# Attention and a two-layer feed-forward on one core: the weights' low bits on GpSimd, sums of |v| in six operations, a later output scale, and a new order of the first units

## The chip, the cores and the metric

The kernel runs on one core of a Trainium2 chip. The metric is the device time of one execution in microseconds (us). The kernel before took 600.85 us in the median of 3 runs (599.13 to 602.35). All data starts and ends in the device's HBM; the host only lays the arrays out.

The core has TensorE for matrix products (PE in the profile; PEld is the loading of its stationary operand), VectorE (DVE), ScalarE (ACT), GpSimd (POOL) and SyncE (SP), which issues the DMAs here. Each engine works through its own list of instructions in order; semaphores tie the lists together.

## The reference, cut to what matters

```python
scores = scale * q @ k.T                         # batch 4, heads 8, sequence 768, head size 64
keep = is_global | is_local                      # keys 0..7, and the last 96 positions
scores = where(keep, scores - slope[h] * dist, -1e9)
a = softmax(scores)
x = (a @ v) laid out as (4 * 768, 512)
h = x @ w_in                                     # 512 x 2048
g = maximum(h, 0) + alpha * minimum(h, 0)
out = g @ w_out                                  # 2048 x 512, float32
```

All inputs arrive as float32, but the two weight matrices are float64 in memory and the kernel makes its own operands of them. To keep float32's precision with 16-bit products, an operand is split into a high and a low float16 part, and a product is three matmuls: high by high, high by low, low by high.

## The kernel before, in words

**Units.** The 3072 tokens are 12 units of 256 tokens (u = 0 to 11, three for each batch entry b). A unit goes through attention for eight heads (`attend`), a transposition of its result x (`x_transpose`) and the feed-forward over 16 blocks f of 128 hidden columns: `ff_in` makes h and from it g in a high part gh and a low part gl, `ff_out` adds g's product to the output. Units 0 and 1 compute their attention in float32 (`score_pair`, and transposes on TensorE); later units split q, k, v and the probabilities and transpose through DMAs (`load_pair`, `split_pair`, `load_v`). Units 4 to 11 take the first product two blocks by two with seven products in place of eight (`seven`), out of sums of weight blocks that `sum_w` makes once.

**Weights.** `load_w` fetches the float64 words of a block f in two DMAs of 512 KB, and `split_w` turns each into a high and a low float16 part. The step touched by the change is in the middle of `split_w`. A float64 word has 64 bits; a float32 word is joined of its high half, shifted by three, and of the three bits below, which lie at the top of the low half. ScalarE makes two 16-bit halves of a tile `wb`: the upper from the word's high half (L576), the lower from bits of its low half (L578: a multiplication by 2 to the -13, with a constant tile `floor` as the bias so that the conversion to a whole number rounds down). VectorE joins them with the high half by a shift and an exclusive or (L583), into `wf` or, for the blocks that `sum_w` needs, into `words`. Then the float16 high part is rounded (L588 on VectorE, L587 on ScalarE, as the planner chooses), and the low part is what is left (L402). This happens 32 times, all in the first fifth of the kernel. Later every word is read again (`load_again`, `sizes`): a check that the weights lie in the range for which the splitting is made. It feeds `check` at the end, and if it fails, a general version runs.

**Scales.** For each batch entry `v_load`, `v_sums`, `v_most` and `v_range` bound the attention's result: a sum of |v| over the columns, the largest over the partitions (by a product on TensorE), and out of its exponent two powers of two: `vs`, by which x is scaled before it is split (L519 to L522), and `osc`, by which the output is scaled (L523 to L525). For b = 0 the sums are three reductions on VectorE of 1024 columns into two sums each (L486); for later b they are on ScalarE (L491).

**Order.** Nothing in the order is left to the run. Each operation has a key, its priority, in steps of one block f of a late unit (16 steps to a unit), and one or more ways: an engine, an estimated cost and the instructions. `Plan.order` simulates the five engines with these costs, picks on each free engine the ready operation with the lowest key, and lets an engine take an operation that is first another's when the queue there is longer than `FLEX` times its own cost. Buffers are given out in the order of keys. SP's operations are DMAs, with a cost of bytes / 330 per ns. The result is emitted as one fixed list for each engine. So a changed cost or key moves work all over the kernel. Keys that matter here: a unit's feed-forward block has `slot(u, f)`, its heads begin at `begin(u)` and follow each other by `step(u)`, the transposition comes `XAFTER` behind the last head, a weight's loads and splits lie `WL` and `WLEAD` before its first use, the second reading begins at `AGAIN`. `keep_busy` issues matmuls whose result nobody reads, at three places in the first units.

Of the kernel before, what the change touches and what calls it, by code (L numbers as in the profile page):

```python
# [146 lines left out]
class Plan:  # L147
# [37 lines left out]
    def order(self):  # L185
# [34 lines left out]
        while events:  # L220
# [11 lines left out]
            for e in engines:  # L232
# [28 lines left out]
                if isinstance(cost, Two) and free["POOL"] > now:  # L261
                    cost += SHARE * min(cost, free["POOL"] - now)
                if e == "SP":
                    dma = max(dma, now + 1125) + cost

                    busy, end = now + 525, dma
                    if self.way[i].__name__ == "transposes":
                        busy, end = now + 1245, dma + 500
                else:
                    end = busy = now + cost  # L270
# [25 lines left out]
def c_dve(n, fast=False, ptr=0):  # L296
    return (0.521 if fast else 1.042) * n + 68 + 57 * ptr
# [17 lines left out]
WIDE = 1  # L315
KP = 2
DP = 3.5
FLEX = {'ACT': 1, 'DVE': 1.5, 'POOL': 1}
GROUP = (2, 2, 2, 2)
# [6 lines left out]
WL = 3  # L326
WLEAD = 8
VS = 5
VL = 4
WARM = 9  # L330
FILL = 4
CHECK = 183
ENDING = 4
AGAIN = 60
LATE = 2000
# [7 lines left out]
SLOW, SLOWER = 1.06, 1.02  # L343
V1S, V1M, V1R = 5.5, 3, 1
STEP4 = 1.5
XAFTER = 3
# [9 lines left out]
def fast(tc, cn, a):  # L356
    nc = tc.nc
    ctx = ExitStack()
    with ctx:
# [101 lines left out]
        fin = fixed("fin", [P, 5])  # L461
        floor = fixed("floor", [P, 1])
        ends = fixed("ends", [P, 3, 512], F16)
        op("POOL", -100, 100, lambda: nc.gpsimd.memset(fin.t, 0.0), w=[fin])
        op("POOL", -100, 100, lambda: nc.gpsimd.memset(floor.t, 2.0**-14 - 0.5), w=[floor])
        op("POOL", -100, 1500, lambda: nc.gpsimd.memset(ends.t, 0.5), w=[ends])
# [12 lines left out]
        def v_sums(b, i, key):  # L479
# [4 lines left out]
            if not b:  # L484
                if i % 2 == 0:
                    op("DVE", key, c_dve(1024), lambda: v.tensor_reduce(  # L486
                        out=m.t[:, i : i + 2], in_=t.t, axis=AX.X, op=ALU.add, apply_absolute_value=True), r=[t], w=[(m, i)])
                return
# [18 lines left out]
        def v_range(b, key):  # L507
# [9 lines left out]
            def scale():  # L517
                big, x = e.t[:, 1:2].bitcast(I32), e.t[:, 2:3].bitcast(I32)
                v.tensor_scalar(out=x, in0=big, scalar1=23, scalar2=None, op0=ALU.logical_shift_right)  # L519
                v.tensor_scalar(out=x, in0=x, scalar1=-1, scalar2=266, op0=ALU.mult, op1=ALU.add)  # L520
                v.tensor_scalar(out=x, in0=x, scalar1=220, scalar2=None, op0=ALU.min)
                v.tensor_scalar(out=vs[b].t.bitcast(I32), in0=x, scalar1=23, scalar2=None, op0=ALU.logical_shift_left)  # L522
                v.tensor_scalar(out=x, in0=x, scalar1=-1, scalar2=254, op0=ALU.mult, op1=ALU.add)  # L523
                v.tensor_scalar(out=osc[b].t.bitcast(I32), in0=x, scalar1=23, scalar2=None, op0=ALU.logical_shift_left)
                v.tensor_scalar(out=osc[b].t, in0=osc[b].t, scalar1=1.0 / (WI * WO * KG), scalar2=None, op0=ALU.mult)  # L525

            op("DVE", key, 1150, scale, r=[e], w=[vs[b], osc[b]])

# [28 lines left out]
        def split_w(f, key):  # L557
# [3 lines left out]
            for part, raw in enumerate(raww[f]):  # L561
# [3 lines left out]
                else:  # L565
# [11 lines left out]
                    out=half(1), in_=hi_().bitcast(F32), mul=-(2.0**-60)), r=[raw], w=[(bits, 0)])  # L577
                op("ACT", k, c_act(n) + 209, lambda raw=raw, half=half: nc.scalar.activation(  # L578
                    out=half(0), in_=raw.t.bitcast(U16).rearrange("p (n t) -> p n t", t=4)[:, :, 1], func=AF.Identity,
                    bias=floor.t, scale=2.0**-13), r=[raw, floor], w=[(bits, 1)])  # L580
                wp = (w, f // 2 % 2) if kept else w
# [57 lines left out]

        def keep_busy(out):  # L640

            for n in range(FILL):
                nc.tensor.matmul(out[:, :P], lhsT=ident, rhs=ident, start=True, stop=True)
# [102 lines left out]
        def score_pair(u, h, key):  # L746
# [5 lines left out]
            def scores():  # L752
                if (u, h) == (1, 0):
                    keep_busy(sps[0].t)
                for qb, off, n, _, pc in windows(u):
# [4 lines left out]

            op("PE", key, 5 * 216 + 250 if u % 3 else 950, scores, r=[first[u, h][0]], w=sps)

        def attend(u, h, key):
# [50 lines left out]
            if plain:  # L814
# [13 lines left out]
                used = [pt, rv]  # L828
                cost = 207 * nb
            else:  # L830
# [84 lines left out]
        def x_transpose(u, qb, key):  # L915
# [28 lines left out]
            op("PE", key, 436, transposes, r=[xn[u]], w=[tp])  # L944
            if u == 0 and qb:
                x = buf("h", "busy", [P, UT])
                op("PE", key + 0.01, FILL * 214, lambda: keep_busy(x.t), r=[xn[u]], w=[x])
            mul(key, lambda: y.t[:, :NC, cols], tv, vs[0], [tp, vs[0]], [(y, qb)], "ACT", 512, True)
# [148 lines left out]
        def ff_out(u, f, key):  # L1097
# [6 lines left out]
            for t, half in ((0, None), (1, 0), (1, 1)) if u == NU - 1 else ((0, None), (1, None)):  # L1104
# [3 lines left out]
                def products(t=t, o=o, cols=cols):  # L1108
                    if u == f == t == 0:
                        keep_busy(o.t)  # L1110
                    tok = slice(128 * t, 128 * t + 128)
# [52 lines left out]
        for h in range(0, H, 2):  # L1164
            jobs.append((-90, load_first, (0, h)))
            jobs.append((-60 + h / 8, load_first, (1, h)))
        for u in range(NU):
# [17 lines left out]
        for f in range(NF):  # L1185
            jobs.append((2 * f - WL - WLEAD if f >= 8 else f - 61, load_w, (f,)))
            jobs.append((2 * f - WL, split_w, (f,)))
# [172 lines left out]
```

## Time and profile before

| | us |
|---|---|
| three runs, median (lowest to highest) | 600.85 (599.13 to 602.35) |
| the profiled execution, its own time | 601.47 |
| its span, first to last instruction | 599.7 |
| TensorE busy | 582.2 |
| VectorE busy | 500.6 |
| ScalarE busy | 421.3 |
| GpSimd busy | 82.3 |

The profile is of one execution. "Busy" is the time in which an engine has at least one instruction under way; matmuls are pipelined, and their ends are modelled, so a busy TensorE need not be at its peak. The granted clock is TensorE's, as a share of the full 2.4 GHz.

### The profile page before, as it was taken

What the parts mean: (1) busy time and instruction counts of PE and PEld (TensorE: products, weight loads), DVE (VectorE), ACT (ScalarE), POOL (GpSimd) and SP (SyncE); (2) the same over time, 40 slices, a digit from 0 to 9 for tenths busy, and PEclk for the clock granted to TensorE, in tenths of its full rate; (3) what the DMA queues carried; (4) which work ended last, traced back from release to release, by engine and by line L of the source; (5) the groups of instructions that cost most, each with busy time, mean ns of one, the idle gap of its engine ahead of it and who ended that gap; (6) DMA issues with size and microseconds to landing.
All of it is one profiled execution on the core that took longest, in us unless ns stands there. A gap on an engine that the chain in (4) does not pass through costs nothing.

```text
span 599.7 us, 16469 instructions
## 1 busy us (share of the span) xinstructions
PE 582.2 (97%) x6324; PEld 422.1 (70%) x6324; DVE 500.6 (83%) x1380; ACT 421.3 (70%) x1054; POOL 82.3 (14%) x161
## 2 busy tenths in 40 slices
PE   8899999999999999999999999999999999999995
PEld 6787666766766666677777777776677777777783
DVE  7899999997899698889879878889889878776442
ACT  6899999978788688767667667766667666641311
POOL 2001232433233332000000000000011000000000
PEclk9899999999999999999999999999999999999999
DMA  8988378257356569669977869588976947521001
GB/s 308 409 357 270 105 243 205 54 111 192 79 137 129 112 155 262 162 173 178 227 178 169 224 164 162 129 229 149 239 173 142 226 94 98 92 52 26 36 3 41
DMA packets 138919, 97.39 MB, mean 162 GB/s; under 512 B 115536, under 2 KB 115792, under 8 KB 138832
## 3 DMA queue, kind: packets, MB, share of 16 engines
q1 hardware_dynamic: 138832, 96.26, 65.0%
q8 instruction: 51, 0.84, 0.6%
q14 instruction: 36, 0.29, 0.2%
HBM read 58.22 MB, written 6.29 MB: 108 GB/s over the span
## 4 chain that ended last, share of the span: by engine, by line
PE 72%; DVE 16%; ACT 5%; DMA 3%; issue 3%; POOL 1%; SPq 0%; ACTq 0%; POOLq 0%; DVEq 0%
PE o L1113 32%; PE ha L1051 11%; PE hc L1051 8%; PE h L964 8%; PE av L863 5%; PE sp L741 3%; DVE pr L785 2%; ACT pr L795 2%; DMA xt<-xs 2%; DVE ps L402 1%; DVE ws L1008 1%; PE sp L758 1%; PE tp L820 1%; DVE g L977 1%; DMA raw<-in_qk_dram 1%
## 5 line engine op out<-in xcount | busy, mean ns | idle before, releaser
L1113 PE MATMUL o<-whl,gh 128*128 128x512 f16 (+1 forms) x800 | 230.2, 371 | 0.3 <-ACT os L1134 0.3
L1113 PE MATMUL o<-whl,gl 128*128 128x512 f16 (+1 forms) x400 | 148.2, 371 | 0.6 <-POOL gl L401 0.2
L1113 PEld LDWEIGHTS <-gh 128*128 128x128 f16 x800 | 71.5, 98 | 50.5 <-issue 3.3
L795 ACT ACTIVATE pr<-pr,sm 128x256 f32<-128x256 f32 (+1 forms) x176 | 85.5, 489 | 22.8 <-DVE sm L785 22.1
L1051 PEld LDWEIGHTS <-sw 128*128 128x128 f16 x1536 | 91.4, 98 | 12.0 <-issue 2.2
L964 PE MATMUL h<-xt,whl 128*128 128x256 f16 x768 | 92.8, 273 | 1.2 <-DVE g L977 0.7
L964 PEld LDWEIGHTS <-whl 128*128 128x128 f16 x768 | 74.4, 98 | 20.4 <-issue 3.2
L1051 PEld LDWEIGHTS <-whl 128*128 128x128 f16 x1152 | 70.9, 98 | 15.5 <-issue 1.9
L785 DVE CUSTOM_DVE_ANT_0 pr<-sp,D 128x256 f32<-128x256 f32 (+1 forms) x192 | 69.4, 393 | 6.2 <-PE sp L758 3.0
L1113 PEld LDWEIGHTS <-gl 128*128 128x128 f16 x400 | 39.1, 98 | 46.7 <-POOL gl L401 2.9
L401 POOL TENSOR_TENSOR gl<-g,gh 128x256 f16<-128x256 f32 x59 | 52.3, 886 | 110.7 <-ACT gh L979 103.2
L402 DVE SCALAR_TENSOR_TENSOR ps<-pr,ps 128x512 f16<-128x512 f32 (+1 forms) x80 | 56.4, 706 | 3.0 <-ACT ps L375 2.9
L1051 PE MATMUL ha<-xt,whl 128*128 128x128 f16 x768 | 53.2, 219 | 1.1 <-DVE gb L1062 0.8
L1051 PE MATMUL hc<-xt,sw 128*128 128x128 f16 x768 | 53.3, 219 | 0.5 <-DVE ga L1062 0.4
L1051 PE MATMUL ha<-xt,sw 128*128 128x128 f16 x768 | 53.4, 219 | 0.0
L803 POOL TENSOR_TENSOR fin<-fin,sm 128x4 f32<-128x4 f32 x40 | 11.9, 298 | 285.1 <-ACT pr L795 284.9
L375 ACT ACTIVATE ps<-pr 128x512 f16<-128x512 f32 (+1 forms) x77 | 44.8, 591 | 6.3 <-DMA pt<-ps 6.1
L375 ACT ACTIVATE gh<-ga 128x512 f16<-128x512 f32 x32 | 20.1, 628 | 39.8 <-DVE ga L1090 39.7
L863 PEld LDWEIGHTS <-pt 128*128 128x128 f16 x888 | 30.8, 98 | 5.4 <-issue 1.6
L375 ACT ACTIVATE x<-raw 128x672 f16<-128x672 f32 (+1 forms) x36 | 25.9, 726 | 11.6 <-PE sp L741 10.4
L795 ACT ACTIVATION_READ_ACCUMULATOR pr<-pr,sm 128x1 f32 x176 | 33.9, 192 | 0.0
L402 DVE SCALAR_TENSOR_TENSOR x<-raw,x 128x672 f16<-128x672 f32 (+1 forms) x40 | 33.3, 833 | 0.0
(150 smaller groups left out, 948.5 us busy)
## 6 DMA issues: line engine op xcount, KB each, us to landing
w<-in_w_dram SPq DMA_DIRECT2D x32, 512.0 KB, 8.9
again<-in_w_dram SPq DMA_DIRECT2D x32, 512.0 KB, 5.4
raw<-in_qk_dram SPq DMA_DIRECT2D x28, 336.0 KB, 3.6
out_dram<-os SPq DMA_DIRECT2D x23, 256.0 KB, 2.7
rawv<-in_v_dram SPq DMA_DIRECT2D x9, 512.0 KB, 5.4
raw<-in_qk_dram SPq DMA_DIRECT2D x12, 272.0 KB, 4.0
gp<-v SPq DMA_DIRECT2D x15, 192.0 KB, 3.1
first<-in_first_dram SPq DMA_DIRECT2D x4, 467.0 KB, 5.0
```

Of the source, the lines that this page charges most:

```text
L375: lambda: nc.scalar.mul(out=out(), in_=src(), mul=by.t if tile_ else by)),
L401: return e.tensor_tensor(out=out(), in0=src(), in1=hi(), op=ALU.subtract)
L402: return e.scalar_tensor_tensor(out=out(), in0=src(), scalar=val(), in1=hi(), op0=ALU.mult, op1=ALU.subtract)
L741: nc.tensor.matmul(sps[2 * n + i].t[:, pc : pc + m], lhsT=x.t[rows, qi, 128 * qb : 128 * qb + 128], rhs=x.t[rows, ki, 256 + off : 256 + of ...
L758: nc.tensor.matmul(sps[i].t[:, pc : pc + n], lhsT=qk_[:, 128 * qb : 128 * qb + 128], rhs=qk_[:, 256 + off : 256 + off + n], start=True, st ...
L785: op("DVE", key, c_dve(n) + 10, lambda qb=qb, n=n, dc=dc, pc=pc: v.tensor_tensor_reduce(out=pr.t[:, pc : pc + n], in0=sp.t[:, pc : pc + n] ...
L795: op("ACT", key + 1, c_act(n, ptr=1) + 93, lambda qb=qb, n=n, pc=pc: nc.scalar.activation(out=pr.t[:, pc : pc + n], in_=pr.t[:, pc : pc + ...
L803: op("POOL", key + 3, c_pool(2 * G), lambda: nc.gpsimd.tensor_tensor(out=fin.t[:, : 2 * G], in0=fin.t[:, : 2 * G], in1=sm.t[:, 2 * G : 4 * ...
L863: nc.tensor.matmul(out, lhsT=p_[:, 128 * j : 128 * j + 128], rhs=v_(j), start=m == 0, stop=m == len(ps) - 1)
L964: nc.tensor.matmul(hp.t, lhsT=w.t[:, wi, wc], rhs=x.t[:, NC * xi + c, :], start=n == 0, stop=n == 3 * NC - 1)
L1051: nc.tensor.matmul(out, lhsT=weight(name, f, wi, c), rhs=x.t[:, 8 * piece + m * xi + 2 * j + c, :], start=start and p == n == 0, stop=n == ...
L1113: nc.tensor.matmul(o.t[:, cols], lhsT=g_()[:, tok], rhs=w.t[:, wi, 512 + cols.start : 512 + cols.stop], start=f == 0 and n == 0, stop=f == ...
```

## The change

The lower halves of the 32 word tiles are made by GpSimd's `tensor_scalar` (a multiplication and a minimum) and no more by ScalarE's activation; the constant tile `floor` goes. The sums of |v| for b = 0 are six reductions of 512 columns into one sum each and no more three of 1024. The three operations that make the output scale become an operation of their own, six steps later in priority. In the planner a DMA ahead of step 20 counts 0.8 of its cost (its transposes excepted), and the costs of the first two units' scores and of their products with v are new. Constants of the order change: the distance of later weights' loads, the second reading of the weights 20 steps later, the spacing of heads from unit 4 on, the lead of the pairs' splitting, the sums of |v| for b = 1, the limit at which VectorE takes over work of ScalarE. `keep_busy` takes its number as an argument, four at each place as before, and the keys of the first loads are written with names of the same values.

```diff
...
                 if e == "SP":
+                    if ops[i][0] < FIRST and self.way[i].__name__ != "transposes":
+                        cost *= FIRST_RATE
                     dma = max(dma, now + 1125) + cost
...
-KP = 2
+KP = 1.5
...
-FLEX = {'ACT': 1, 'DVE': 1.5, 'POOL': 1}
+FLEX = {'ACT': 1, 'DVE': 2, 'POOL': 1}
...
-WLEAD = 8
-VS = 5
+WLEAD = 6
+VS = 6
...
-FILL = 4
+F1, F1S, W0, W0S = -60, 0.125, -61, 1
+CPOOL = 1000
+FILL_S, FILL_B, FILL_O = 4, 4, 4
+FIRST, FIRST_RATE = 20, 0.8
+UNSCALE = 6
...
-AGAIN = 60
+AGAIN = 80
...
-V1S, V1M, V1R = 5.5, 3, 1
-STEP4 = 1.5
+V1S, V1M, V1R = 6.5, 3, 1
+STEP4 = 1.7
...
-                if i % 2 == 0:
-                    op("DVE", key, c_dve(1024), lambda: v.tensor_reduce(
-                        out=m.t[:, i : i + 2], in_=t.t, axis=AX.X, op=ALU.add, apply_absolute_value=True), r=[t], w=[(m, i)])
+                op("DVE", key, c_dve(512), lambda: v.tensor_reduce(
+                    out=m.t[:, i : i + 1], in_=t.t[:, i % 2], axis=AX.X, op=ALU.add, apply_absolute_value=True),
+                   r=[(t, i % 2)], w=[(m, i)])
...
                 v.tensor_scalar(out=vs[b].t.bitcast(I32), in0=x, scalar1=23, scalar2=None, op0=ALU.logical_shift_left)
+
+            def unscale():
+                x = e.t[:, 2:3].bitcast(I32)
                 v.tensor_scalar(out=x, in0=x, scalar1=-1, scalar2=254, op0=ALU.mult, op1=ALU.add)
...
-            op("DVE", key, 1150, scale, r=[e], w=[vs[b], osc[b]])
+            op("DVE", key, 660, scale, r=[e], w=[vs[b], e])
+            op("DVE", key + UNSCALE, 490, unscale, r=[e], w=[osc[b]])
...
-                op("ACT", k, c_act(n) + 209, lambda raw=raw, half=half: nc.scalar.activation(
-                    out=half(0), in_=raw.t.bitcast(U16).rearrange("p (n t) -> p n t", t=4)[:, :, 1], func=AF.Identity,
-                    bias=floor.t, scale=2.0**-13), r=[raw, floor], w=[(bits, 1)])
+                low_ = lambda raw=raw: raw.t.bitcast(U16).rearrange("p (n t) -> p n t", t=4)[:, :, 1]
+                op("POOL", k, CPOOL, lambda low_=low_, half=half: nc.gpsimd.tensor_scalar(
+                    out=half(0), in0=low_(), scalar1=2.0**-13, scalar2=7.0, op0=ALU.mult, op1=ALU.min), r=[raw], w=[(bits, 1)])
...
-            op("PE", key, 5 * 216 + 250 if u % 3 else 950, scores, r=[first[u, h][0]], w=sps)
+            op("PE", key, 1100 + 214 * FILL_S * (u == 1 and h == 0) if u % 3 else 850, scores, r=[first[u, h][0]], w=sps)
...
-                cost = 207 * nb
+                cost = 112 * nb + 20
...
-            jobs.append((2 * f - WL - WLEAD if f >= 8 else f - 61, load_w, (f,)))
+            jobs.append((2 * f - WL - WLEAD if f >= 8 else W0 + W0S * f, load_w, (f,)))
```

## Rows read from the trace of the kernel before

**Rows 1.** Page, part 1, and part 4: the chain's shares by engine

```profile
PE 582.2 (97%) x6324; PEld 422.1 (70%) x6324; DVE 500.6 (83%) x1380; ACT 421.3 (70%) x1054; POOL 82.3 (14%) x161
...
PE 72%; DVE 16%; ACT 5%; DMA 3%; issue 3%; POOL 1%; SPq 0%; ACTq 0%; POOLq 0%; DVEq 0%
```

**Rows 2.** Busy time by stretch, all engines: stretch, length, busy (instructions), clock, DMA

```profile
10.00:30.00 20.00, 17.66 (x136) 15.46 (x136) 16.76 (x69) 17.61 (x41) 0.20 (x1) 0.91 1.03 408
...
50.00:70.00 20.00, 19.14 (x143) 13.02 (x141) 20.00 (x41) 18.89 (x39) 4.42 (x6) 1.00 0.74 240
...
70.00:125.00 55.00, 54.96 (x457) 37.40 (x455) 55.00 (x128) 52.88 (x122) 18.16 (x26) 1.00 0.57 147
...
220.00:250.00 30.00, 28.16 (x322) 20.12 (x321) 27.26 (x77) 26.99 (x77) 6.28 (x11) 1.00 0.97 244
...
590.00:599.70 9.70, 2.28 (x18) 1.57 (x16) 0.48 (x1) 1.13 (x2) 0.00 (x0) 0.87 0.19 63
```

**Rows 3.** Timeline, 26 to 28 us: start, us, engine, line, operation

```profile
26.32 0.15 DVE L523 TENSOR_SCALAR vmm<-vmm 128x1 int32<-128x1 int32 x1
...
26.59 1.13 PE L758 MATMUL sp<-first 64*128 64x256 f32 x8
...
27.16 0.42 DVE L879 TENSOR_TENSOR xn<-av,sm 128x256 f32<-128x256 f32 x1
```

**Rows 4.** Groups by shape, VectorE: count, busy us, mean ns, idle before

```profile
L486 DVE TENSOR_REDUCE vm<-vr 128x2 f32<-128x1024 f32 x3 | 3.6, 1212 | 0.0
```

**Rows 5.** Chain of waits, 11 to 17.3 us: start, us, what

```profile
12.00 0.83 issue
...
13.82 0.85 issue
...
16.24 0.67 ACT wb L576
```

**Rows 6.** Groups by shape, VectorE, 50 to 125 us

```profile
L583 DVE SCALAR_TENSOR_TENSOR wf<-w,wb 128x512 int32<-128x512 int32 x18 | 14.6, 810 | 0.0
...
L402 DVE SCALAR_TENSOR_TENSOR whl<-wf,whl 128x512 f16<-128x512 f32 x17 | 11.6, 687 | 0.0
...
L588 DVE TENSOR_SCALAR whl<-wf 128x512 f16<-128x512 f32 x9 | 4.5, 495 | 0.0
```

**Rows 7.** Busy time by stretch, line L578 alone

```profile
50.00:125.00 75.00, 19.00 (x23) 1.00 0.61 172
...
10.00:50.00 40.00, 8.55 (x10) 0.96 0.92 359
```

**Rows 8.** Line L401 on GpSimd: ns min/median/max, first and last start; who waited

```profile
L401 POOL TENSOR_TENSOR gl<-g,gh x59: 670/842/1327, 49.4 to 232.9; 128x256 f16<-128x256 f32 x59
...
  PEld L1113: 2.9, 6
```

**Rows 9.** Chain of waits, 49 to 67 us: shares by line

```profile
by line: DVE wf L583 28.6%; DVE whl L402 21.3%; issue 13.7%; DVE g L977 9.6%; DVE whl L588 8.3%; DVE words L583 6.7%; DVE xt L402 4.1%; PE h L964 3.3%; DVE gl L981 2.2%; PE av L863 0.7%; DVE sm L785 0.4%; DVE x L376 0.4%; DVE g L376 0.4%; D
```

**Rows 10.** Timeline, 58.5 to 59 us, VectorE and GpSimd

```profile
58.95 1.18 DVE L583 SCALAR_TENSOR_TENSOR wf<-w,wb 128x512 int32<-128x512 int32 x1
...
58.91 0.67 POOL L401 TENSOR_TENSOR gl<-g,gh 128x256 f16<-128x256 f32 x1 [2.30 <-ACT gh L979]
```

**Rows 11.** Line L583: duration in ns min/median/max

```profile
L583 DVE SCALAR_TENSOR_TENSOR wf<-w,wb x24: 654/684/1179, 18.0 to 122.8; 128x512 int32<-128x512 int32 x24
```

**Rows 12.** Tile xt's products on TensorE, and line L604

```profile
L1051 PE MATMUL ha<-xt,whl x768: 216/219/220, 231.5 to 585.5; 128*128 128x128 f16 x192
...
L604 ACT ACTIVATE size<-again x32: 661/675/691, 233.1 to 537.6; 128x512 f16<-128x512 f32 x32
```

**Rows 13.** Chain of waits, 212 to 246 us

```profile
233.11 0.66 ACT size L604
```

**Rows 14.** Chain of waits and timeline, 398 to 412 us

```profile
398.73 9.20 DMA xt<-xs
...
411.80 0.61 PE L1051 MATMUL ha<-xt,whl 128*128 128x128 f16 x8
```

More of the change, by code (lines that the diff above doesn't have):

```diff
@@ L461, in fast @@
         fin = fixed("fin", [P, 5])
-        floor = fixed("floor", [P, 1])
         ends = fixed("ends", [P, 3, 512], F16)
         op("POOL", -100, 100, lambda: nc.gpsimd.memset(fin.t, 0.0), w=[fin])
-        op("POOL", -100, 100, lambda: nc.gpsimd.memset(floor.t, 2.0**-14 - 0.5), w=[floor])
         op("POOL", -100, 1500, lambda: nc.gpsimd.memset(ends.t, 0.5), w=[ends])
@@ L638, in load_first, with keep_busy @@
                     firstv[u, h + i] = x, (lambda i=i: x.t[:, nk + 195 * i : nk + 195 * i + 195])
-        def keep_busy(out):
-            for n in range(FILL):
+        def keep_busy(out, fill):
+            for n in range(fill):
                 nc.tensor.matmul(out[:, :P], lhsT=ident, rhs=ident, start=True, stop=True)
@@ L753, in scores @@
                 if (u, h) == (1, 0):
-                    keep_busy(sps[0].t)
+                    keep_busy(sps[0].t, FILL_S)
                 for qb, off, n, _, pc in windows(u):
@@ L944, in x_transpose @@
             op("PE", key, 436, transposes, r=[xn[u]], w=[tp])
-            if u == 0 and qb:
+            if u == 0 and qb and FILL_B:
                 x = buf("h", "busy", [P, UT])
-                op("PE", key + 0.01, FILL * 214, lambda: keep_busy(x.t), r=[xn[u]], w=[x])
+                op("PE", key + 0.01, FILL_B * 214, lambda: keep_busy(x.t, FILL_B), r=[xn[u]], w=[x])
             mul(key, lambda: y.t[:, :NC, cols], tv, vs[0], [tp, vs[0]], [(y, qb)], "ACT", 512, True)
@@ L1109, in products @@
                     if u == f == t == 0:
-                        keep_busy(o.t)
+                        keep_busy(o.t, FILL_O)
                     tok = slice(128 * t, 128 * t + 128)
@@ L1165, in fast @@
             jobs.append((-90, load_first, (0, h)))
-            jobs.append((-60 + h / 8, load_first, (1, h)))
+            jobs.append((F1 + F1S * h, load_first, (1, h)))
         for u in range(NU):
```

## The prediction

> **What bounds the kernel now.** I read the page's busy shares first, then the busy time by stretch, then the chain of waits where TensorE is not full, and last the groups of the operations that the change touches. TensorE is busy 97% of the span, VectorE 83%, ScalarE 70%, GpSimd 14%, and the chain that ended last lies for 72% on TensorE [rows 1]. So time can be won only where TensorE waits or runs slowly, and the table by stretch shows where [rows 2]. From 10 to 30 us TensorE is idle 20 - 17.66 = 2.34 us, and its mean granted clock is 0.91: part of the stretch is at 1.2 and not 2.4 GHz, which costs about 0.09 x 20 = 1.8 us of full-speed work. From 50 to 70 it is idle 0.86 us, from 220 to 250 1.84, and 7.42 from 590 on, where the last outputs are evicted and written, which the change leaves alone. From 70 to 125 it is idle 0.04 us although VectorE is busy 55.00 of 55 and ScalarE 52.88: both vector engines are full there, yet TensorE always has something queued. This is the trap of the change: it unloads ScalarE mostly in a stretch where TensorE hardly waits.
>
> **The change part by part.** All sums are against the profiled execution's own 601.47 us (span 599.7 and 1.77 around it). It lies 0.62 above the median, 600.85; the same difference is taken off both.
>
> *The output scale later.* Three small operations (L523 to L525, 0.15 us each, from 26.32) stand on VectorE between the scale of v and what makes the first block ready for its transposes: 0.45 us leave that line [rows 3]. But the transposes wait for xn (27.16 + 0.42 = 27.58) and also for TensorE itself, which has the scores until 26.59 + 1.13 = 27.72 [rows 3]. The scores are the cover; worth 0 to 0.45, and I take 0.1, since xn ends only 0.14 before TensorE is free and 0.45 earlier would count only where the scores come earlier too.
>
> *Sums in six operations.* Three reductions of 1024 columns take 1212 ns each [rows 4]. In the chain two small operations sit behind such a reduction, for 0.83 and 0.85 us [rows 5]. Between halves a waiting operation can go in. No reduction of 512 columns is in the trace; half of 1212 is 606, and a two-input operation on 512 columns takes 684 in the median [rows 11], so six take 3.64 to 4.10 us against 3.64: up to 0.46 us more, in a stretch where VectorE is busy 16.76 of 20 us. If both waits shrink by half, 0.84 is gained; if both halves still run together, 0.46 is lost. I take 0.6 gained, near the rows of the chain, because each half is now a step of its own for the planner.
>
> *The low bits on GpSimd.* 32 operations leave ScalarE, 27.55 us in all: 8.55 (10 operations) from 10 to 50 and 19.00 (23, one cut by the edge) from 50 to 125 [rows 7]. GpSimd ran no such operation. Its subtraction with two inputs of 256 columns reads as many elements and takes 670 ns at least, 842 in the median [rows 8]; were an input of 512 columns as dear as two of them, 1684. So 0.67 to 1.68 us each; I take 1.0, near the median of the row, 32 us on an engine that is busy 82 of 600. The chain through a word gets no longer, for the operation now runs beside ScalarE's high half, which it followed before. Behind it on GpSimd queues the subtraction that makes gl, which TensorE reads 3.5 steps of the order later in the first units; all waits of TensorE's weight loads for gl are now 2.9 us [rows 8]. So I cost it at nothing; if those steps are not enough, each of some 25 subtractions in the stretch can be late by 1.0 us.
>
> Early, from 10 to 30, ScalarE is busy 17.61 of 20 us [rows 2], and TensorE loses 2.34 in idling and 1.8 in clock, 4.1 together. The low bits are part of what holds ScalarE up, but where the chain shows ScalarE's split, 0.67 us before the transposes of 17.28, it is the *high* half, L576 [rows 5], which stays. I give this part and the sums together half of the 4.1, 2.0 us: 0.6 above and 1.4 here. Bounds 0 and 3.5.
>
> From 50 to 70 the chain is on VectorE: joining the words (L583) is 28.6% of it and the rest of the split (L402) 21.3% [rows 9]. ScalarE's room helps there only where VectorE hands work over: nine roundings of the split (L588) of 4.5 us in all [rows 6] are free to go to ScalarE. Against this stands what GpSimd costs VectorE. The joining takes 684 ns in the median [rows 11] but 810 in the mean from 50 to 125 [rows 6], and the one that began at 58.95, just behind a subtraction of 0.67 us on GpSimd, took 1.18, 0.50 more [rows 10]. 18 x 0.126 = 2.3 us on 4.42 + 18.16 = 22.6 us of GpSimd [rows 2] is 0.10 us of VectorE for each us of GpSimd, the lower bound; 0.50 / 0.67 = 0.74 is the upper. 23 us more of GpSimd then cost VectorE 2.3 to 17 us; I take 0.25, or 5.8, nearer to the mean of many than to the single case. Hand-over and stretching nearly cancel on VectorE; what is left is ScalarE being earlier with its own. TensorE loses 0.9 us there, of which I take 0.6; bounds 0.9 gained and 6 lost.
>
> The Trainium skill, "GPSIMD Engine Reference", section "Specifications", says that GpSimd shares its SBUF interfaces with VectorE and contends with its instructions that have two SBUF inputs or run in a two-port mode: a rule against this change. The trace agrees for the joining (810 against 684 ns) and not for the rest of the split, which has two inputs as well and takes 687 in the mean [rows 6]. Section "Elementwise — side-by-side cycle accounting" of that page has 769 ns for 512 elements in the best case; by it GpSimd's part would be an estimated 25 us and not 32, and the stretching 4.4 and not 5.8.
>
> *The order.* The moved constants reach every unit. The second reading of the weights starts 20 steps later. A step is (585.5 - 231.5) / 127 = 2.79 us: from the first product of a seven-product unit to the last of the last one are seven units of 16 steps and 15 more [rows 12]. So 56 us later go 32 pairs of a 512 KB DMA on SP and an operation of 675 ns on ScalarE, with two on VectorE behind each. They start today at 233.1 [rows 12], just where the kernel goes over to seven products; the first of them is 0.66 us of the chain [rows 13], three of them fall in that stretch, 2.0 us of a ScalarE that is busy 26.99 of 30, with the DMA share at 0.97 [rows 2]. With them gone I take two thirds of TensorE's 1.84 us idle, 1.2; bounds 0 and 1.84. They come back at the end, when ScalarE is not needed much; a loss there would need the check of the weights to end after the last product. The heads of later units are spaced 1.7 instead of 1.5 steps, and their blocks are transposed 1.6 steps, 4.5 us, later. One such transfer now ends at 398.73 + 9.20 = 407.93, and its unit's products begin at 411.80 [rows 14]: 3.9 us of cover. 0.6 us a unit, 5 in eight, would show if no product of the unit before were left to fill in; I take 0, and 3 lost as the bound. The raw pairs are asked for half a step nearer to their use, and the loads of the later weights two steps; both pass the transposes in SP's queue at places that I can't see from here, so 0, with 1 us either way.
>
> The sum: 0.1 + 0.6 + 1.4 + 0.6 + 1.2 = 3.9 us; 601.47 - 3.9 = 597.6, and from the median 600.85 - 3.9 = 597.0.
>
> **The rivals.**
> *Nothing that can be measured.* (Within 0.5%, about 3 us, a measurement of this kernel can't be told from no change.) ScalarE's room falls where TensorE idles 0.04 us, later transposes take back the 1.2, and the first and second part alone are left, 0.7: 600.2. For it speaks the 97% on TensorE, against it the 4.1 us lost before 30.
> *A larger gain.* "Busy" may hide half-empty stretches. From 70 to 125 TensorE ran 457 matmuls, 8.3 per us; at that rate the 136 of 10 to 30 are 16.4 us and the 143 of 50 to 70 are 17.2 [rows 2]: 3.6 and 2.8 us lost, with the 1.84 at 220 together 8.2, though shapes differ. Three quarters of it are 6.2: 594.7.
> *Slower, by VectorE.* From 50 to 125 VectorE is full, 75.00 of 75 us [rows 2]. If GpSimd stretches it midway between the bounds, 0.42 for each us, its line ends 23 x 0.42 = 9.7 us later, and if the roundings stay on it, TensorE runs dry behind it by as much; the 3.3 us of the head and of 220 to 250 remain: 600.85 + 9.7 - 3.3 = 607.2. It decides from where the stretching less what is handed over exceeds 3.3 us. For it: the rows of the joining. Against it: the rest of the split shows no stretch [rows 6].
>
> **How the numbers follow.** Forecast 0.49, its own range 595.3 to 598.7; nothing 0.28; larger gain 0.12; slower 0.11. The range of 592.8 to 602.5 takes in the first three nearly whole and leaves out the slower case and a tail of the larger gain. Faster than 597.85 are the larger gain and 0.38 of the forecast's 0.49: 0.50. Slower than 603.85 is most of the slower case: 0.10. The rest is 0.40.
>
> **What would show it.** Right: ScalarE's total some 27 us lower and GpSimd's 32 higher [rows 1]; TensorE's idle time from 10 to 30 below 1.5 us with its clock above 0.91, and from 220 to 250 below 1 us; the mean of the joinings still above 800 ns, with fewer roundings on VectorE. Wrong: low bits above 1.4 us on GpSimd; TensorE idle by over 2 us between 50 and 125; the first product of a late unit waiting for a transposed block.

## The result: 0.8% slower, and the profile after

The changed kernel takes 605.37 us in the median of five runs (604.08 to 605.79), the kernel before 599.77 on the same chip; the ratio is 1.008, with an interval of 1.0055 to 1.0106. The forecast was 597.0 with a range to 602.5. It was wrong, on the side to which it gave 0.10. The profiled execution is one of 605.65 us, with a span of 603.9. Three single executions of the experiments below, of 670, 672 and 861 us at mean granted clocks of 0.85, 0.85 and 0.65, stand in no ratio.

First the page of the changed kernel, parts 1 and 4, to be laid beside [rows 1]:

```profile
PE 583.5 (97%) x6324; PEld 422.6 (70%) x6324; DVE 502.3 (83%) x1366; ACT 412.0 (68%) x1047; POOL 151.2 (25%) x184
...
PE 69%; DVE 14%; ACT 4%; issue 3%; POOL 1%; DMA 1%; DVEq 0%; ACTq 0%; POOLq 0%
```

GpSimd has gained 68.9 us, and not 32. ScalarE has lost 9.3, although 27.5 were taken from it; it has 1047 instructions for 1054, with 32 moved away, so the planner gave it 25 others. The moved operation itself, by its line (ns min/median/max, first and last start; below it who waited, us and times):

```profile
L587 POOL TENSOR_SCALAR wb<-w x32: 2095/2225/2621, 14.6 to 121.2; 128x512 uint16<-128x512 uint16 x32
...
  DVE wf L591: 3.8, 3
```

On ScalarE it took 861 ns (27.55 us for 32). The busy time by stretch (stretch, length, busy and count on PE, PEld, DVE, ACT, POOL, then clock, DMA share and GB/s), beside [rows 2]:

```profile
10.00:30.00 20.00, 18.52 (x144) 15.68 (x141) 17.63 (x75) 17.02 (x43) 9.58 (x6) 0.91 1.03 408
50.00:70.00 20.00, 16.50 (x101) 10.78 (x99) 15.42 (x26) 14.26 (x30) 18.41 (x10) 0.83 0.39 132
70.00:125.00 55.00, 51.84 (x435) 34.47 (x434) 54.13 (x116) 48.21 (x120) 50.80 (x35) 1.00 0.58 161
220.00:250.00 30.00, 29.19 (x316) 20.71 (x315) 27.31 (x74) 26.70 (x72) 9.57 (x14) 1.00 0.66 169
```

From 50 to 125 GpSimd is now the full engine: 69.21 of 75 us, 92%. VectorE, full before, is idle for 5.45 us. TensorE is idle for 3.50 + 3.16 = 6.66 us where it was idle for 0.90. At 10 to 30 it gained 0.86 us of idling and at 220 to 250 it gained 1.03. How far the work has come is read from the first product of unit 4 (beside [rows 12]; the second line is the second reading of the weights):

```profile
L1059 PE MATMUL ha<-xt,whl x768: 216/219/230, 239.1 to 591.0; 128*128 128x128 f16 x192
...
L612 ACT ACTIVATE size<-again x32: 655/676/688, 295.8 to 584.6; 128x512 f16<-128x512 f32 x32
```

Unit 4 begins at 239.1 instead of 231.5, 7.6 us late; from there to the end of the span it is 603.9 - 239.1 = 364.8 us instead of 599.7 - 231.5 = 368.2, 3.4 less. So the change loses early what it only half regains later.

Where the early loss arises is seen in the chain of waits of the changed kernel, here from 48 to 61 us and, below the second gap, from 88 to 94 (start, us, what; "issue" is time in which the engine waited for nothing that the profile shows):

```profile
48.43 2.29 POOL wb L587
50.72 0.35 issue
51.07 0.70 POOL wb L587
51.77 1.99 issue
53.76 1.01 POOL gl L407
...
54.82 1.89 PE o L1121 x4
56.71 4.71 PE h L972 x24
...
87.94 2.12 POOL wb L587
90.08 0.69 DVE wf L591
...
93.58 0.34 DVE g L985
```

The subtraction that makes `gl` stands behind low bits on GpSimd's fixed list; its timeline has three of them in a row before it:

```profile
45.91 7.77 POOL L587 TENSOR_SCALAR wb<-w 128x512 uint16<-128x512 uint16 x3 [0.77 <-DMA w<-in_w_dram]
53.76 1.00 POOL L407 TENSOR_TENSOR gl<-g,gh 128x256 f16<-128x256 f32 x1
```

The `gh` that it needs is ready at 50.67 (ScalarE's conversion of 0.41 us from 50.26), so `gl` is 3.1 us late. TensorE's own list has nothing before that product, and the next view, TensorE's timeline, shows the wait of 3.50 us and what follows it:

```profile
54.82 0.61 PE L1121 MATMUL o<-whl,gl 128*128 128x512 f16 x1 [3.50 <-POOL gl L407]
...
56.50 4.91 PE L972 MATMUL h<-xt,whl 128*128 128x256 f16 x24
...
62.54 2.78 PE L972 MATMUL h<-xt,whl 128*128 128x256 f16 x24
```

The same 24 matmuls take 4.91 us behind the wait and 2.78 later: the clock was at 1.2 GHz there (granted clock from 55 to 60 us: 0.50), and the mean from 50 to 70 is 0.83.

There is a second path. VectorE, which has to join the words and has a fixed list as well, stood idle for 0.86 us before the joining at 90.08 until the low bits were there. What TensorE needs of VectorE comes later by that, too: at 93.97 it has waited 1.57 us for `g`. Over the whole kernel TensorE's matmuls waited for (us, times, longest):

```profile
PE o L1121 <- POOL gl L407: 4.5, 4, 3.5
...
PE h L972 <- DVE g L985: 1.9, 2, 1.6
```

Of the 6.66 us from 50 to 125, 3.7 are waits for `gl` and 2.9 waits for VectorE.

### The profile page after: what moved, and what is told of

It is laid out like the page before. It is cut to its first block, busy times and chain, and to the rows that moved or that the text cites. A ratio compares the mean times of both kernels' runs of the same rounds, so it can differ in the third digit from the quotient of the medians.

```text
span 603.9 us, 16515 instructions
## 1 busy us (share of the span) xinstructions
PE 583.5 (97%) x6324; PEld 422.6 (70%) x6324; DVE 502.3 (83%) x1366; ACT 412.0 (68%) x1047; POOL 151.2 (25%) x184
## 4 chain that ended last, share of the span: by engine, by line
PE 69%; DVE 14%; ACT 4%; issue 3%; POOL 1%; DMA 1%; DVEq 0%; ACTq 0%; POOLq 0%
PE o L1121 33%; PE ha L1059 13%; PE hc L1059 10%; PE h L972 6%; PE av L871 3%; PE sp L749 3%; DVE whl L408 2%; DVE ps L408 1%; DMA xt<-xs 1%; DVE wf L591 1%; DVE g L985 1%; ACT pr L803 1%; DVE x L408 1%; DVE pr L793 1%; DVE ws L1016 1%
## 5 line engine op out<-in xcount | busy, mean ns | idle before, releaser
L803 ACT ACTIVATE pr<-pr,sm 128x256 f32<-128x256 f32 (+1 forms) x176 | 85.8, 490 | 17.3 <-DVE sm L793 16.8
L972 PE MATMUL h<-xt,whl 128*128 128x256 f16 x768 | 94.3, 276 | 2.0 <-DVE g L985 1.9
L811 POOL TENSOR_TENSOR fin<-fin,sm 128x4 f32<-128x4 f32 x40 | 14.6, 366 | 284.4 <-ACT pr L803 284.4
L587 POOL TENSOR_SCALAR wb<-w 128x512 uint16<-128x512 uint16 x32 | 73.8, 2307 | 19.9 <-DMA w<-in_w_dram 7.8
L407 POOL TENSOR_TENSOR gl<-g,gh 128x256 f16<-128x256 f32 x51 | 45.4, 892 | 61.6 <-ACT gh L987 47.9
L408 DVE SCALAR_TENSOR_TENSOR ps<-pr,ps 128x512 f16<-128x512 f32 (+1 forms) x80 | 55.0, 689 | 2.0 <-ACT ps L381 1.8
L381 ACT ACTIVATE ps<-pr 128x512 f16<-128x512 f32 (+1 forms) x78 | 46.4, 597 | 3.9 <-DMA pt<-ps 3.6
L381 ACT ACTIVATE g<-h,ak 128x256 f32<-128x256 f32 x60 | 27.8, 465 | 12.5 <-PE h L972 12.3
L985 DVE SCALAR_TENSOR_TENSOR g<-h,g 128x256 f32<-128x256 f32 x64 | 26.4, 414 | 10.5 <-ACT g L381 10.5
```

Of the source, the lines that this page charges most:

```text
L381: lambda: nc.scalar.mul(out=out(), in_=src(), mul=by.t if tile_ else by)),
L407: return e.tensor_tensor(out=out(), in0=src(), in1=hi(), op=ALU.subtract)
L408: return e.scalar_tensor_tensor(out=out(), in0=src(), scalar=val(), in1=hi(), op0=ALU.mult, op1=ALU.subtract)
L587: op("POOL", k, CPOOL, lambda low_=low_, half=half: nc.gpsimd.tensor_scalar(out=half(0), in0=low_(), scalar1=2.0**-13, scalar2=7.0, op0=AL ...
L803: op("ACT", key + 1, c_act(n, ptr=1) + 93, lambda qb=qb, n=n, pc=pc: nc.scalar.activation(out=pr.t[:, pc : pc + n], in_=pr.t[:, pc : pc + ...
L972: nc.tensor.matmul(hp.t, lhsT=w.t[:, wi, wc], rhs=x.t[:, NC * xi + c, :], start=n == 0, stop=n == 3 * NC - 1)
```

## Experiments

Ratios are to the kernel before, run on the same chip; the interval is 95%. The kernel before had medians of 599.77 to 599.93.

**Low bits back on ScalarE (all else as changed).**

```diff
-                op("POOL", k, CPOOL, ... nc.gpsimd.tensor_scalar(
+                op("ACT", k, c_act(n) + 209, ... nc.scalar.activation(
```

> The changed kernel with the low bits back on ScalarE; the six sums, the later output scale and all constants of the order stay. Theory 1 (the price of the operation: GpSimd takes 2.3 us for what the planner counts as 1.0, and is the bound from 50 to 125 us): the 6.7 us of TensorE's idle time from 50 to 125 fall to about 1, and the time to 596 to 601. Theory 2 (the new order itself is worse): it stays at 603 to 606, TensorE idle at the same places or others.

599.24 us, 0.9994 (0.9978 to 1.0009). With the low bits back the whole loss, 6.1 us to this kernel, is gone. All the rest of the change together is worth nothing that can be measured. Its stretches 10 to 30, 50 to 70 and 70 to 125:

```profile
10.00:30.00 20.00, 17.62 (x145) 15.00 (x145) 16.90 (x77) 17.73 (x47) 0.19 (x1) 1.00 1.03 409
50.00:70.00 20.00, 18.06 (x134) 11.98 (x131) 20.00 (x42) 19.61 (x38) 5.90 (x5) 1.00 0.65 218
70.00:125.00 55.00, 53.20 (x445) 36.24 (x443) 53.98 (x126) 52.23 (x121) 16.39 (x26) 1.00 0.60 159
```

TensorE's idle time from 50 to 125 is 3.74 us and not the 1 expected, so 2.8 of the 5.8 that the changed kernel adds are here too, in the new order with the low bits on ScalarE. They cost little: unit 4 begins at 232.7, 1.2 us later than before.

**Low bits on GpSimd alone, in the kernel before.**

```diff
-                op("ACT", k, c_act(n) + 209, ... nc.scalar.activation(
+                op("POOL", k, CPOOL, ... nc.gpsimd.tensor_scalar(
```

> The kernel before with one thing of the change: the low bits on GpSimd, counted as 1.0 us. Theory 1: slower by 4 to 8 us, 604 to 608, with GpSimd busy over 90% somewhere between 50 and 125 us. Theory 2: 599 to 601, as before.

610.95 us, 1.0196 (1.0166 to 1.0227), above the 604 to 608 expected: with the old constants the move costs twice as much. The operation takes 2314 ns, and the two stretches are:

```profile
50.00:70.00 20.00, 15.39 (x114) 10.84 (x113) 17.42 (x27) 15.21 (x31) 19.27 (x10) 1.00 0.48 159
70.00:125.00 55.00, 50.20 (x424) 33.36 (x422) 52.08 (x112) 40.88 (x102) 48.22 (x34) 1.00 0.53 143
```

TensorE is idle for 9.41 us at a full clock, with GpSimd busy for 67.49 of 75 us and VectorE idle for 5.5. Over this kernel its matmuls wait 4.2 us for VectorE's `g` and 2.4 for `gl`.

**The planner told the measured price.**

```diff
-CPOOL = 1000
+CPOOL = 2300
```

> The changed kernel with one number changed: the planner counts 2300 and not 1000 for the operation on GpSimd. If the loss comes from the planner's wrong count (lists of the engines in an order that GpSimd can't keep), it shrinks by half or more: 599 to 602. If GpSimd simply has too much to do from 15 to 125 us (74 us of low bits and 25 us of gl in 110), it stays at 603 to 606. Theory 2: 603 to 606 as well.

604.69 us, 1.0062 (1.0028 to 1.0096), but this is no single value: four runs of 599.2 to 599.8 at a mean granted clock of 0.998, two between, and five of 605.7 to 607.7 at 0.985 to 0.988. The gap goes with the clock: (0.998 - 0.986) x 605 = 7.3 us of full-speed work. Which of the two brings the other is not shown; in the changed kernel 605.37 us goes with a clock of 0.995 and 605.79 with 0.988. In the execution profiled, 599.70 us:

```profile
50.00:70.00 20.00, 17.94 (x134) 12.10 (x132) 18.40 (x37) 18.64 (x42) 18.80 (x9) 1.00 0.80 268
70.00:125.00 55.00, 52.70 (x437) 35.26 (x435) 54.39 (x115) 43.43 (x108) 50.13 (x36) 1.00 0.56 161
```

GpSimd is as full as in the changed kernel, yet TensorE is idle for 4.36 us and not 6.66: its matmuls wait 2.4 us for `gl` in place of 4.5. So in its better runs this kernel is rid of the loss with as much work on GpSimd, in another list, and there the wrong price in the planner is a part of the loss. In the median that is not shown: 604.69 lies in the 603 to 606 of the second case, five runs are as slow as the changed kernel, and the interval overlaps with that of its 1.008.

> The third experiment's kernel once more, for a second profile: its runs fell apart into 599 and 606, and the profile was of 599.7. If GpSimd's load lets TensorE's clock fall in some runs and not in others: a run near 606 shows stretches at the lower clock of some 13 us more than the 4.1 us at the end of the first profile, or a run near 599 shows none again.

One more execution of the same kernel took 599.12 us at 0.997, again with no stretch at the lower clock before the last outputs. No run near 606 has a profile, so what lets the clock fall in some of them stays open.

**What makes the operation dear.** The kernel goes through six forms in turn: as it is; input adjacent; 32-bit output; one operation and not two; both of the first two; float32 to float16. Most forms make other numbers than the reference; the one execution took 610.60 us.

```diff
+                if kind == 1:
+                    low_ = lambda raw=raw: raw.t.bitcast(U16)[:, :n]
...
+                if kind == 3:
+                    extra = dict(scalar2=None)
```

> What makes the operation dear: the changed kernel with six forms of it in turn over the 32 places (weights come out wrong in five of them). Form 0 as it is; 1 reads adjacent 16-bit numbers and not every fourth; 2 writes adjacent 32-bit numbers and not every second 16-bit one; 3 has one operation, the multiplication, in place of two; 4 is 1 and 2 together; 5 is float32 in, every second, to float16, one operation. If the stride of 16-bit numbers costs it, forms 1, 2 or 4 take 1.0 us or less; if the second operation, form 3 does; if neither, all take over 1.8 us.

GpSimd's groups by shape (count, busy us, mean ns, idle before); the first holds as it is, adjacent and one operation, the second the two with 32-bit output, the third the float form:

```profile
L602 POOL TENSOR_SCALAR wb<-w 128x512 uint16<-128x512 uint16 x17 | 37.3, 2194 | 14.1 <-DMA w<-in_w_dram 8.3 <-DMA raw<-in_qk_dram 2.8 <-DVE sm L834 1.0
L602 POOL TENSOR_SCALAR wb<-w 128x512 int32<-128x512 uint16 x10 | 20.5, 2050 | 1.4 <-ACT wb L584 0.7
L602 POOL TENSOR_SCALAR wb<-w 128x512 f16<-128x512 f32 x5 | 9.3, 1861 | 1.4 <-issue 1.1
```

By the single instructions, five or six of a form, the medians are 2.43 us as it is, 2.48 with adjacent input, 1.75 with one operation, 2.01 and 1.92 with 32-bit output (the second with adjacent input too), and 1.72 in the float form, which has one operation. So the second operation is the largest part that can be taken off, 0.68 us; an output of adjacent 32-bit numbers takes off 0.4 to 0.5, and adjacent input at most 0.1. No form comes near 1.0. The planner's own formula for GpSimd, 340 + 3.0 x 512 = 1876 ns, was nearer than the 1000 written in.

**The length of the operation alone.** Two kernels with the same lists: GpSimd's operation follows ScalarE's, which writes the whole word instead of its upper half (so the weights are wrong throughout, in both); only the columns that GpSimd reads differ, 184 or 512.

```diff
-                    out=half(1), in_=hi_().bitcast(F32), mul=-(2.0**-60)), r=[raw], w=[(bits, 0)])
+                    out=bits.t.bitcast(F32), in_=hi_().bitcast(F32), mul=-(2.0**-60)), r=[raw], w=[(bits, 0)])
...
-                    out=half(0), in0=low_(), ..., r=[raw], w=[(bits, 1)])
+                    out=half(0)[:, :SHORT], in0=low_()[:, :SHORT], ..., r=[raw, (bits, 0)], w=[(bits, 1)])
```

> The changed kernel with the low bits made for 184 of 512 columns (the others keep bits of the high half's float32, so the weights come out slightly wrong), which should take about 1.0 us on GpSimd, what the planner counts. For this ScalarE writes whole 32-bit words and GpSimd works behind it, not beside it; all lists are those of the next kernel. If the length of the operation is the whole error: joinings done by 124 us and not 129, TensorE idle under 2 us from 50 to 125, and 595 to 599, as forecast (3.9 us below before). If the use of GpSimd itself (its hold on VectorE, waits between engines) is a part: 600 to 604.

> The same lists with all 512 columns, 2.3 us each, behind ScalarE. As the changed kernel or worse, since the two halves now follow each other: 605 to 610. If it is at 600 or below, the order of this pair differs from the changed kernel's and the pair says nothing on it.

The short one takes 598.62 us, 0.9985 (0.9969 to 1.0), the full one 620.62, 1.0349 (1.0324 to 1.0374), more than the 605 to 610 expected. In the short one the last joining starts at 119.5 us, as expected, but TensorE is idle for 3.74 us from 50 to 125, as long as in the first experiment's kernel, and not for under 2. The short kernel's operation and its products of unit 4:

```profile
L588 POOL TENSOR_SCALAR wb<-w 128x184 uint16<-128x184 uint16 x32 | 34.3, 1072 | 36.1 <-ACT wb L585 27.5 <-DVE sm L794 4.4 <-DVE ps L409 2.7
...
L1060 PE MATMUL ha<-xt,whl x768: 216/219/229, 231.8 to 583.4; 128*128 128x128 f16 x192
```

and the full one's, with the line of h's product on TensorE (idle time before it at the end) and the wait for low bits before VectorE's work on tile `wf` (us, times):

```profile
L588 POOL TENSOR_SCALAR wb<-w 128x512 uint16<-128x512 uint16 x32 | 76.7, 2397 | 23.4 <-ACT wb L585 21.1 <-DVE vmm L526 0.4
...
L1060 PE MATMUL ha<-xt,whl x768: 216/219/229, 253.6 to 605.1; 128*128 128x128 f16 x192
...
L973 PE MATMUL h<-xt,whl 128*128 128x256 f16 x768 | 94.4, 276 | 9.3 <-DVE g L986 8.7
...
  POOL wb L588: 17.5, 16
```

With nothing but 32 x (2397 - 1072) = 42.4 us more on GpSimd, unit 4 begins 21.8 us later and the time is 22.0 us longer. In this form the loss is larger than in the changed kernel, where the operation runs beside ScalarE's, and the second path is the longer one: VectorE waits 17.5 us for low bits and TensorE 8.7 for VectorE's `g`, but only 3.4 for `gl`. The pair also says what the change would have been at the price that I forecast, in this form: 0.9 us faster than before (0 to 1.9), not 3.9.

**Is it the clock? TensorE kept busy in the wait.** 60 matmuls with zeros, which leave the sums as they are, are put where TensorE waits for `gl` at 51 us.

```diff
+                        if (u, f, t) == (0, 2, 0) and n in (0, 2):
+                            nothing(0 if n == 0 else 60)
```

> The changed kernel with 60 matmuls of a tile of zeros (128 columns, added to the output's sum, so that nothing changes in it) on TensorE between the two halves of the product that waits 3.5 us for gl at 51 to 55 us. All other lists are the same. If the 6.8 us at the lower clock from 54.0 are a price of that wait, and cost as much as they look (6.8 us at half speed, 3.4 us of work): the clock stays up there and the time falls by about 3, to 602. If the lower clock is hidden by later waits for GpSimd: 604.5 to 605.5 as before, with the clock up.

```profile
50.00:70.00 20.00, 17.93 (x170) 13.10 (x169) 16.25 (x27) 14.85 (x31) 19.28 (x10) 1.00 0.41 140
70.00:125.00 55.00, 51.34 (x421) 33.97 (x421) 53.53 (x115) 47.99 (x120) 50.74 (x36) 1.00 0.59 161
```

The clock stays at 1.00 there, and in this execution from 10 to 30 us too. The kernel takes 606.0 us, 1.0111 (1.0093 to 1.0129), no less than without. So the lost clock of the changed kernel is no term of its loss: unit 4 begins at 239.3 with the full clock and at 239.1 without.

**Fewer low bits on GpSimd.** Half of them, and then all with a free choice (ScalarE first, GpSimd at 2300), of which the planner gave GpSimd 12; and the second with 42 zero matmuls.

```diff
+                if not part:
+                  op("POOL", k, CPOOL, ...
+                else:
+                  op("ACT", k, c_act(n) + 209, ...
```

```diff
+                plan.op(k, [raw, floor], [(bits, 1)],
+                        ("ACT", c_act(n) + 209, ...),
+                        ("POOL", CPOOL, ...))
```

> The third experiment's kernel (2300 counted) with half the low bits back on ScalarE: 16 operations, one of a block's two, stay on GpSimd. Theory 1 (GpSimd has too much to do): its busy share from 50 to 125 falls from 92% to about 60%, the runs no longer fall apart into 599 and 606, and the time is 596 to 600. If any use of GpSimd there costs, by holding VectorE or by making TensorE's clock fall: 601 to 605.

> The low bits first on ScalarE, and on GpSimd (counted 2300) where ScalarE's queue is longer than that; the planner gives 12 of 32 to GpSimd. All else as changed. Theory 1: the best of the kernels, 596 to 599, with ScalarE below 52 of 55 us from 70 to 125 and GpSimd below 70%. If ScalarE's room is worth nothing there, as the first experiment's equal time suggests: 598.5 to 600.5.

> The kernel of the seventh experiment (12 of the low bits on GpSimd, the planner's choice) with 14 and 28 such matmuls of zeros in the same product, where it waits 0.9 and 1.6 us. If its 3.4 us at the lower clock from 56.6 cost 1.7 us: 597.7 against its 599.3, and so faster than the kernel before. If not: 599 to 600.

599.76, 599.32 and 599.44 us: 0.9994 (0.998 to 1.0008), 0.9992 (0.9979 to 1.0004) and 0.9998 (0.9986 to 1.001). With 16 of them GpSimd is busy 46.91 of 75 us (63%), and the loss is gone; but there is no gain either. ScalarE's room is worth nothing that can be measured here, at either dose, and the filled waits give nothing back.

**Sums and output scale alone, in the kernel before.**

```diff
+                op("DVE", key, c_dve(512), lambda: v.tensor_reduce(
+                    out=m.t[:, i : i + 1], in_=t.t[:, i % 2], ...
...
+            op("DVE", key + UNSCALE, 490, unscale, r=[e], w=[osc[b]])
```

> The kernel before with two things of the change: the six sums and the later output scale (the planner orders anew with these alone). By the prediction's steps 0.7 us faster, 599.2 against 599.9, with the clock from 10 to 30 us at 0.91 or above. If the pieces matter only through a new order, anything within 1.5 us of before either way.

601.44 us, 1.0023 (1.0004 to 1.0041), not the gain of 0.7. In the execution profiled, of 602.54 us, the clock from 10 to 30 is 0.83, below the 0.91 of before, and TensorE is idle there for 1.77 us instead of 2.34. Its runs part by the granted clock too: three of 598.3 to 598.7 at 0.997, nine of 600.7 to 603.3 at 0.991 to 0.993. The six reductions take 680 ns each, 4.0 us together.

**The second reading of the weights.** Back to step 60 in the first of these experiments' kernels (low bits on ScalarE), and to step 80 in the kernel before.

```diff
-AGAIN = 80
+AGAIN = 60
```

```diff
-AGAIN = 60
+AGAIN = 80
```

> The first experiment's kernel (low bits on ScalarE) with the second reading of the weights at its old place, step 60 and not 80. By the prediction's step it loses 1.2 us against that kernel, 600.4 and not 599.2, with TensorE's idle time from 220 to 250 us back from 0.9 to about 1.8. If the later reading is worth nothing: 599.2, idle time there about 0.9.

> The kernel before with one constant of the change, the second reading of the weights at step 80. By the pair of the first and eighth experiments (601.7 at 60, 599.2 at 80) about 2 us faster: 597.5 to 598.5. If the later reading is only worth something together with the other constants: 599.3 to 600.5.

The first: 601.70 us, 1.0032 (1.0017 to 1.0046), 2.5 above the kernel with 80. The second: 598.01, 0.9975 (0.996 to 0.999), 1.5 us faster than before. From 220 to 250 us, the stretch named for it, the kernel before with 80 has TensorE idle for 0.23 us in place of 1.84:

```profile
220.00:250.00 30.00, 29.77 (x337) 21.49 (x335) 27.98 (x78) 27.09 (x80) 7.95 (x14) 1.00 0.74 170
```

In the other pair the gain lies elsewhere. The first experiment's kernel, with step 80, and the same with 60:

```profile
220.00:250.00 30.00, 29.10 (x329) 21.37 (x328) 26.74 (x78) 27.76 (x81) 8.22 (x14) 1.00 0.62 137
250.00:590.00 340.00, 339.88 (x4209) 249.03 (x4206) 277.03 (x777) 207.19 (x534) 16.20 (x48) 1.00 0.66 148
...
220.00:250.00 30.00, 28.55 (x327) 20.94 (x325) 27.56 (x80) 27.08 (x78) 6.96 (x12) 1.00 0.83 197
250.00:590.00 340.00, 337.68 (x4190) 246.75 (x4188) 275.76 (x777) 205.69 (x534) 16.90 (x50) 1.00 0.66 141
```

TensorE is idle for 1.45 us and not 0.90 from 220 to 250, but for 2.32 and not 0.12 from 250 to 590.

**A version that beats both.** At step 80 with 3.5 steps between readings the last three of the 32 get keys behind the step that takes the maximum over all of them: in the changed kernel that maximum is taken at 564.9 us and the last comparison comes at 585.7. So the kernel's check of the weights' range leaves out the last three tiles, a fault of the change that its time does not show. The spacing is brought down so that all 32 lie before it.

```diff
-AGAIN = 60
+AGAIN = 80
...
-RATE = 3.5
+RATE = 3.15
```

> The kernel before with the second reading of the weights from step 80 on, each 3.15 and not 3.5 steps after the last, so that its last comparison lies at step 181.7, ahead of the check at 183. As the eleventh experiment, 597.5 to 598.5, and 1 to 2 us faster than before. If the closer spacing costs ScalarE or the DMAs something: 599 to 600.

596.61 us (594.65 to 597.15), 0.9938 (0.9913 to 0.9963), 3.3 us faster than before where 1 to 2 were expected. The last operation of its second reading on ScalarE starts at 555.0, and unit 4 to the end takes 595.4 - 232.5 = 362.9 us:

```profile
L1051 PE MATMUL ha<-xt,whl x768: 216/219/230, 232.5 to 582.5; 128*128 128x128 f16 x192
...
L604 ACT ACTIVATE size<-again x32: 652/672/684, 288.4 to 555.0; 128x512 f16<-128x512 f32 x32
```

## Why the prediction was wrong

*The step that failed* is the price of the low bits: "So 0.67 to 1.68 us each; I take 1.0". They took 2.31 in the mean, 2.10 at least, above the upper bound. Both bounds came from a subtraction with two inputs of 256 columns. The reading behind the lower one and behind the 1.0, that the cost goes by the elements read, was false: one input of 512 columns costs 2.1 to 2.6 us with two operations and about 1.75 with one (the six forms). The upper one, 842 x 2 = 1684, goes by the elements written; it is close for one operation, and the 0.68 us of the second was left out. The Trainium skill, "GPSIMD Engine Reference", section "Elementwise — side-by-side cycle accounting", has 769 ns for 512 elements in the best case; the trace has 2307, so that for this operation the measurement decides against it.

*"So I cost it at nothing"* fell with the price. 74 us of low bits must pass GpSimd between 14.6 and 124 us, with `gl` behind them in the same list. The cover of 3.5 steps was gone: TensorE's weight loads wait for `gl` for 7.1 us, where it was 2.9 [rows 8], and its matmuls for 4.5, where it was 0.2. The sentence itself had the mechanism ("each of some 25 subtractions in the stretch can be late by 1.0 us") and left it out of the sum and of the rivals. The second path, VectorE waiting in its own list for low bits (3.8 us here, 17.5 in the kernel with 512 columns behind ScalarE), is in no step of the prediction. That the length of the operation is enough for a loss is shown by the pair with 184 and 512 columns; that the planner's 1000 makes part of it, only by the better runs of the kernel with 2300, which are level with before. Both signs that I had named for this, low bits above 1.4 us and TensorE idle by over 2 us from 50 to 125, came.

*VectorE stretched by GpSimd*, the rival on the slower side, had the sign and not the mechanism. It wanted joinings slower and VectorE full. The groups on VectorE from 50 to 125 us, beside [rows 6]:

```profile
L591 DVE SCALAR_TENSOR_TENSOR wf<-w,wb 128x512 int32<-128x512 int32 x17 | 13.1, 774 | 4.1 <-POOL wb L587 3.8 <-ACT wb L584 0.3
L408 DVE SCALAR_TENSOR_TENSOR whl<-wf,whl 128x512 f16<-128x512 f32 x17 | 12.9, 768 | 0.1
...
L596 DVE TENSOR_SCALAR whl<-wf 128x512 f16<-128x512 f32 x4 | 2.4, 607 | 0.0
```

With three times the work on GpSimd (69.21 us, not 22.58) the joining takes 774 ns, less than the 810 of before; the rest of the split rises from 687 to 768 and the rounding from 495 to 607. So the means show no stretching of the joining and 17 x 0.081 = 1.4 us for the split, and VectorE now waits 3.8 us for the low bits. The test that I had written, joinings still above 800, came out against me; fewer roundings on VectorE, 4 for 9, came out right.

The single instructions of the two traces say what the means hide. Without an operation of GpSimd beside it, no joining into `wf` and no rest of its split took over 0.70 us in either kernel. Beside one, five of 10 joinings took 1.10 to 1.18 us before, and in the changed kernel three of 21 took over 1.0. The rest of the split ran beside GpSimd in 7 of 24 cases before, one of them of 0.83 us, and in 23 of 24 after, seven of them of 0.88 to 1.15. So the split had seemed unstretched in [rows 6] because it seldom met GpSimd, and my price for each us of GpSimd, 0.10 to 0.74, does not carry over from one of its operations to another.

*ScalarE's room, 1.4 + 0.6 us.* TensorE's idle time from 10 to 30 did fall below 1.5 (to 1.48), but the clock stayed at 0.91. With the low bits still on ScalarE the first experiment's kernel had a clock of 1.00 there, with 2.38 us idle, so the 1.8 us for the clock did not hang on the low bits. With 12, 16 or 32 cheaper low bits away from ScalarE no kernel shows a gain beyond 0.9 us. The opening remark, that the change unloads ScalarE where TensorE hardly waits, should have been given more weight than the busy shares of the head.

*The sums and the output scale, 0.7 us.* Not shown: alone they measure 1.4 slower, in runs that differ by the granted clock. Their size, up to 0.46 us more on VectorE, was right (4.0 us for 3.64). "No reduction of 512 columns is in the trace" was not: L539 of the kernel before is one, of float16, and took 675 ns, near the 680 measured.

*The later second reading, 1.2 us.* Right in sign and too small: TensorE's idle time at 220 to 250 fell to 0.81, and the step is worth 1.5 to 2.5. The place was right for the kernel before; in the new order most of the gain lies behind 250 us. *Later heads at nothing* held: with the reading back at 60 and all other constants moved, unit 4 to the end takes 600.2 - 232.2 = 368.0 us, and 368.2 before.

The sum as measured, in the two executions profiled: 7.6 us lost before unit 4 and 3.4 won behind it, 4.2 of span (the medians of the five runs are 5.6 apart).

## What to carry to other kernels

An operation that an engine has never run in the trace has no price from a row that resembles it in elements; where another operation stands behind it on a full path, the rival "this engine becomes the bound" is to be worked out above the upper price too (here 2.31 us for 1.68), with the operations on other engines that wait for its result. Before moving work off an engine ask whether the engine that everything waits for is idle in that very stretch: here it was for 0.9 us of 75, and no more could be won there at any price. A wrong price in a planner can cost twice, in the engine's time and in a list that puts the urgent operation behind the dear one; the second is shown here for the better runs of one kernel only.

## What the runs showed of the hardware

- GpSimd's `tensor_scalar` on 512 columns took 1.75 us with one operation in the median (1.72 from float32 to float16) and 2.1 to 2.6 with two, from and to strided 16-bit numbers; with adjacent 32-bit output and two operations 1.92 to 2.01; on 184 columns, with two, 1.07 in the mean.
- VectorE's joinings and splits of 512 columns took 0.67 to 0.69 us in the kernels before and after whenever no operation of GpSimd ran beside them, and up to 1.18 beside one, though many of these took no longer.
- Runs of one program part by TensorE's granted clock: 599 us at 0.998 against 606 at 0.985 to 0.988 for the kernel with 2300, 598 at 0.997 against 601 to 603 at 0.991 to 0.993 for the sums alone. In the changed kernel it fell to 1.2 GHz at a wait of 3.5 us, and that fall cost nothing that can be measured, as the filled wait shows.
